# Spreading the softmax's inverse sums by TensorE transposes of a widened copy instead of broadcast DMAs

## The chip, the cores and the metric

The kernel runs on one core of a Trainium2 chip. The metric is device time in microseconds (us) of one execution; for the kernel before, the median of three runs is 564.24 us (563.70 to 567.82). Profiles are single executions recorded by the hardware profiler. PE is TensorE's matmul row and PEld its weight loads, DVE is VectorE, ACT ScalarE, POOL GpSimd, SP SyncE (here it only issues DMAs; SPq is its queue).

## The reference

An attention with a window feeds a gated feed-forward block (FFN). There are 4 batches, 8 heads, 768 positions, head width 64; a query sees the 8 first keys and the 96 last ones.

```python
scores = scale * q @ k.T + bias          # bias: -slope of the head * distance
scores = where(keep, scores, -1e9)
a = exp(scores - max(scores))
a = a / (sum(a) + 1e-9)
x = a @ v                                # heads side by side: [4, 768, 512]
h = relu(x @ w_in)                       # 512 -> 1024
gate = sigmoid(conv3(h))                 # three taps along the positions, per channel
out = (h * gate) @ w_out                 # 1024 -> 512
```

What the change touches is the division by the row sums. The kernel does not divide `a`; it multiplies the product with `v` by the inverse sums. That product stands with the 64 columns of a head on the partitions and the queries along the free axis, so the inverse sums, which come out one per partition (one per query), must be turned, and repeated over 64 partitions.

## The kernel before, in words

**Jobs and steps.** A job `m` is one batch, one half `u` of the positions (384 queries) and one pair of heads: 32 jobs. A job has NB = 3 steps of 128 queries, so there are 96 steps `s`. Four jobs make one FFN stage `n` (8 stages of 384 positions).

**One step of attention.** `scores` (L373) multiplies queries and keys on TensorE into a bank of PSUM (pool `ps_s`, three banks). `maxima` (L408) adds the bias and takes the extremes on DVE. `exps` (L425) takes exponentials on ACT, with the sums of the rows in `sums[m]`. Two steps later (LAG_T) `transposes` (L454) turns the exponentials on TensorE into a bank of pool `ps_t` (one bank), and ACT copies them to SBUF (L464 to L467). After a job's third step `inverses` (L436) adds 1e-9 and takes reciprocals on DVE (128x6). `spread` (L441) transposes these 6 columns on TensorE (L443), copies the 6 rows to SBUF on ACT (`row`, L445) and issues six DMAs from SP (L449), each of which writes one row of 128 numbers to 64 partitions of `rs`. `values` (L470), three steps after a job's last (LAG_V), does 24 small matmuls with `v` (L475), then multiplies by `rs` on DVE (L486) and splits the result into a rounded part `xh` on ACT (L487) and the rest `xl` on POOL (L488). The FFN's first matmuls read those.

**FFN work.** `ffn(n)` (L637) makes a list of items: 24 of `mm1` (four matmuls each, L506), 16 or 32 of `mm2` (three each, L619) of the stage before, and between them the work of the other engines (ReLU L517/L519, three taps L555 to L557, tanh L575, a check of saturation L586, gating and split L607 to L610). The main loop (from L751) takes items from that list by `fill`, some before `values` and `transposes` of a step and some behind. How many is set by `left`, the number of steps to spread the rest of the list over (L798). `fill` puts an item behind the scores, maxima and exponentials of the step before, on each engine.

**Order.** Up to step 10 (HAND = 11) the order on every engine is the order of the program. From step 11 on the compiler's list scheduler, which plans with its own durations, orders ACT, DVE, POOL and SP; TensorE keeps the order of the program (L787). Each engine then works its list strictly in order.

**Beside it.** In the first 15 steps (NATIVE = 5 jobs) each of the two heads of a step has a bank of its own for its scores. In the first 31 steps or so the weights are decoded from 8-byte words on DVE (L318 to L322), in pieces given out per step. `load`, `load_v` and `weight_load` issue the inputs' DMAs from SP. `prep` (L122) rounds the keys and queries of jobs from 5 on, on DVE, ACT and POOL (L134 to L145). At the end `check_weights` (L336) reads the weights once more, in 18 pieces, behind the last `xh` (`cur["mixed"]`) on ACT.

Of the kernel before, what the change touches and what calls it, by code (L numbers as in the profile page):

```python
# [67 lines left out]
def fast_path(tc, io):  # L68
# [14 lines left out]
    pg = pool("pg", 4)  # L83
    ps_s = pool("ps_s", 3, space=PSUM)
    ps_t = pool("ps_t", 1, space=PSUM)
    ps_v = pool("ps_v", 1, space=PSUM)
# [6 lines left out]
    def load(m):  # L93
# [5 lines left out]
        if m < NATIVE:  # L99
            rk = p2.tile([P, w // 2], F32, tag="kk", name=f"rk{m}")  # L100
            rq = p2.tile([P, TB], F32, tag="qh", name=f"rq{m}")
            for j in range(2):
                rows = slice(64 * j, 64 * j + 64)
                k0 = 2 * TB + j * NKC[u]
                nc.sync.dma_start(rk[rows], src[rows, k0 : k0 + NKC[u]])
                nc.sync.dma_start(rq[rows], src[rows, j * TB : (j + 1) * TB])
        else:
            rk = p1.tile([P, w], F32, tag="rk", name=f"rk{m}")
            rq = p1.tile([P, 2 * TB], F32, tag="rq", name=f"rq{m}")
            nc.sync.dma_start(rk, src[:, 2 * TB :])  # L110
            nc.sync.dma_start(rq, src[:, : 2 * TB])
# [258 lines left out]
    last_ttr = {}  # L370
    st_s, st_pt, pv, xt, sums, rs, line = {}, {}, {}, {}, {}, {}, {}

    def scores(s):  # L373
# [9 lines left out]
        else:  # L383
            sp = [ps_s.tile([P, 256], F32, tag="s", name=f"s{s}_{j}") for j in range(2)]
        for j in range(2):
# [22 lines left out]
    def maxima(s):  # L408
# [4 lines left out]
        if i == 0:  # L413
            sums[m] = p1.tile([P, 3, 2 * NB], F32, tag="sums", name=f"sums{m}", bufs=3)
        for j in range(2):
# [9 lines left out]
    def exps(s):  # L425
# [3 lines left out]
        for j in range(2):  # L429
            last_exp[s] = A.activation(  # L430
                pb[:, j, c0 : c0 + n], sp[j][:, c0 : c0 + n], AF.Exp,
                bias=mm[:, j : j + 1], scale=-1.0, accum_out=sums[m][:, 0, NB * j + i : NB * j + i + 1],
            )
# [7 lines left out]
    def spread(m):  # L441
        pv[m] = ps_v.tile([P, TB + P], F32, tag="v", name=f"pv{m}")
        T.transpose(pv[m][: 2 * NB, TB:], sums.pop(m)[:, 2], ident)  # L443
        row = p1.tile([2 * NB, P], F32, tag="row", name=f"row{m}")
        A.activation(row, pv[m][: 2 * NB, TB:], AF.Copy)  # L445
        rs[m] = p2.tile([P, TB], F32, tag="rs", name=f"rs{m}")
        for c in range(2 * NB):
            j, i = divmod(c, NB)
            nc.sync.dma_start(  # L449
                rs[m][64 * j : 64 * j + 64, i * P : (i + 1) * P],  # L450
                row[c : c + 1].unsqueeze(1).broadcast_to([1, D, P]),
            )

# [15 lines left out]

    def values(m):  # L470
        for i in range(NB):
            sb, ka = st_pt.pop(NB * m + i)
            for c, n in ((0, ka), (1, P - 24)):
                for j in range(2):
# [5 lines left out]
                        stop=c == 1,  # L480
                    )
        xh = px.tile([P, TB], F32R, tag="xh", name=f"xh{m}")
        xl = px.tile([P, TB], F32R, tag="xl", name=f"xl{m}")
        xt[m] = (xh, xl)
        x = rs.pop(m)
        V.tensor_tensor(x, pv[m][:, :TB], x, ALU.mult)  # L486
        cur["mixed"] = A.activation(xh, x, AF.Copy)  # L487
# [265 lines left out]
    for s in range(len(steps) + LAG_V + 1):  # L753
        cur["s"] = s
        m, i = steps[s] if s < len(steps) else (len(jobs), -1)
        if s < HAND:
            scores(s)
            if ends(s - LAG_V):
                values((s - LAG_V) // NB)
            if s >= LAG_T:  # L760
                transposes(s - LAG_T)
            maxima(s)
            exps(s)
            if i == 0 and m:
                inverses(m - 1)
            elif i == 1 and m:
                spread(m - 1)
# [15 lines left out]
        else:  # L783
            if hand:
                hand = False
                manual.__exit__(None, None, None)
                manual = tc.manual_schedule(engines={mybir.EngineType.PE})  # L787
                manual.__enter__()
            if s < len(steps):
# [5 lines left out]
            if e >= 0:  # L795
                if e % SPU == SPU - 1:
                    queue.extend(ffn(e // SPU))
                left = SPU - (e + 1) % SPU  # L798
                if e + 1 >= len(steps) - SPU:
                    left += 2  # L800
                k = -(-sum(cost for cost, _, _ in queue) // left)
            if s <= len(steps) and i < 1:
                inverses((s - 1) // NB)
            elif s == len(steps) + 1 or i == 1:
                spread(s // NB - 1)
            if s < LAG_V + SPU:
# [3 lines left out]
            if ends(s - LAG_V):  # L810
                values((s - LAG_V) // NB)
            if s < len(steps) + LAG_T:
                transposes(s - LAG_T)
# [7 lines left out]
        if s == 0:  # L821
            for k in range(len(order)):
                chain(*order[k])
        for k, at in enumerate(FIRST_LOADS):
            if at == s:
                start_piece(k)
        if i == 0:
            prep(m + 1, 0)
            prep(m + 1, 1)
            if 1 <= m < NATIVE - 1:  # L830
                load(m + 1)
        elif i == 1 and m + 2 >= NATIVE:
            load(m + 2)
        if s >= 2 and (s - 2 - (LAG_V - 3)) % NB == 0:
            load_v((s - 2 - (LAG_V - 3)) // NB + 1)
    fill(10**9)
# [6 lines left out]
    last_tiles()  # L843
    manual.__exit__(None, None, None)
    if wide:
# [166 lines left out]
```

## Time and profile before

| | |
|---|---|
| median of three runs | 564.24 us (563.70 to 567.82) |
| the profiled execution's own time | 566.89 us |
| its span, first to last instruction | 565.1 us |
| mean granted TensorE clock | 0.914 |
| time around the span | 566.89 - 565.1 = 1.79 us |

The page of the profile gives busy shares of each engine, the chain of work that ended last (followed back from the last instruction, at each step to what released it), and groups of instructions with their busy time, mean duration, the idle time before them and what ended it. Views of the trace give waits by engine and window, busy time by window, and single instructions in order of time. An engine's idle time costs something only when that engine, or what waits for it, sets the end.

### The profile page before, as it was taken

To read this page: it belongs to the slowest core of one execution; us is meant where nothing else is said; L and a number is where in the kernel's file an instruction comes from. 1 tells how busy PE (TensorE), PEld (TensorE's weight loads), DVE (VectorE), ACT (ScalarE), POOL (GpSimd) and SP (SyncE) were. 2 spreads that over 40 slices of the span, in tenths; PEclk is the share of its full clock that TensorE was granted. 3 is DMA by queue.
4 is the path that set the end of the run, shared out by engine and by line. 5 is a ranking of instruction groups with operands and counts; after the bars stand their busy time and mean duration, and the time that the engine had idled before them with its cause. 6 is when DMAs were issued, how large, how long until landed. Compare 5 with 4: busy or idle time off the path is not lost.

```text
span 565.1 us, 9158 instructions
## 1 busy us (share of the span) xinstructions
PE 474.3 (84%) x3045; PEld 405.1 (72%) x3045; DVE 373.5 (66%) x825; ACT 303.9 (54%) x825; POOL 257.9 (46%) x210
## 2 busy tenths in 40 slices
PE   7686686676967899998978899899978899988795
PEld 6464465575965689787867798788867788777584
DVE  5346599996796758754867788557669677137720
ACT  2345475665756556652565646644655487246710
POOL 4023477663873745673554355574534442233000
PEclk8957688887997979998998899999979899999999
DMA  6844876645553644465555654475545534476511
GB/s 193 200 93 106 186 216 181 139 125 127 101 115 22 149 89 96 115 139 117 107 107 108 143 90 81 78 169 127 109 55 129 118 44 78 82 209 197 179 57 43
DMA packets 38328, 68.10 MB, mean 121 GB/s; under 512 B 6145, under 2 KB 19969, under 8 KB 38273
## 3 DMA queue, kind: packets, MB, share of 16 engines
q1 hardware_dynamic: 34816, 61.28, 50.5%
q10 hardware_dynamic: 3456, 6.16, 2.9%
q8 instruction: 26, 0.43, 0.3%
q14 instruction: 30, 0.24, 0.1%
HBM read 54.84 MB, written 6.29 MB: 108 GB/s over the span
## 4 chain that ended last, share of the span: by engine, by line
DMA 22%; DVE 22%; PE 22%; SPq 12%; ACT 11%; issue 8%; POOL 2%; DVEq 0%; ACTq 0%; POOLq 0%
DMA rs<-row 15%; SPq L449 11%; PE h L506 9%; PE o L619 7%; DVE c L557 3%; DMA check<-in_w_in 3%; DVE c L556 3%; ACT pbuf L430 3%; DVE s L418 3%; DVE c L607 2%; DMA check<-in_w_out 2%; DVE rs L486 2%; DVE w L320 2%; ACT sat L586 1%; PE s L399 1%
## 5 line engine op out<-in xcount | busy, mean ns | idle before, releaser
L430 ACT ACTIVATE pbuf<-s,mm 128x232 f32<-128x232 f32 (+1 forms) x192 | 82.1, 433 | 68.5 <-DVE mm L418 66.7
L555 POOL TENSOR_SCALAR c<-hbuf,cw 128x382 f32<-128x382 f32 (+1 forms) x64 | 47.7, 748 | 78.7 <-ACT hbuf L519 41.4
L619 PE MATMUL o<-woh,gh 128*128 128x512 f32 x192 | 82.5, 430 | 0.8 <-ACT hbuf L519 0.7
L418 DVE CUSTOM_DVE_ANT_0 s<-s,tab 128x232 f32<-128x232 f32 (+1 forms) x192 | 73.0, 385 | 15.2 <-PE s L399 8.2
L619 PE MATMUL o<-woh,gl 128*128 128x512 f32 x192 | 78.4, 408 | 2.9 <-DVE gl L610 2.9
L619 PE MATMUL o<-wol,gh 128*128 128x512 f32 x192 | 78.4, 408 | 0.0
L506 PE MATMUL h<-xh,wih 128*128 128x384 f32 x252 | 60.3, 358 | 18.6 <-ACT xh L487 15.0
L460 PE MATMUL t<-ident,pbuf 128*128 128x128 f32 (+1 forms) x192 | 55.6, 311 | 23.7 <-ACT pt L467 17.2
L488 POOL TENSOR_TENSOR xl<-rs,xh 128x384 fp32r<-128x384 f32 x32 | 37.8, 1180 | 81.0 <-ACT xh L487 74.8
L145 POOL TENSOR_TENSOR ql<-rq,qh 128x768 fp32r<-128x768 f32 x24 | 48.3, 2011 | 44.3 <-DVE qh L140 23.8
L143 POOL TENSOR_TENSOR kk<-rk,kk 64x1008 fp32r<-64x1008 f32 (+1 forms) x27 | 61.0, 2260 | 11.8 <-POOL ql L145 4.5
L556 DVE SCALAR_TENSOR_TENSOR c<-hbuf,cw,c 128x382 f32<-128x382 f32 (+1 forms) x64 | 52.0, 815 | 19.6 <-POOL c L555 19.3
L506 PE MATMUL h<-xl,wih 128*128 128x384 f32 x252 | 62.0, 370 | 0.2 <-POOL xl L488 0.2
L506 PEld LDWEIGHTS h<-xh,wih 128*128 128x128 f32 x252 | 45.9, 199 | 22.1 <-ACT xh L487 17.1
L506 PE MATMUL h<-xh,wil 128*128 128x384 f32 x252 | 61.4, 369 | 0.0
L467 ACT ACTIVATE pt<-t 128x512 f32<-128x512 f32 x80 | 47.1, 589 | 22.0 <-PE t L461 22.0
L475 PE MATMUL pv<-pt,v 104*64 104x128 f32 (+2 forms) x768 | 55.1, 289 | 2.4 <-ACT row L445 1.5
L557 DVE SCALAR_TENSOR_TENSOR c<-hbuf,cw,c 128x382 f32<-128x382 f32 (+1 forms) x64 | 54.9, 858 | 0.8
L460 PEld LDWEIGHTS t<-ident,pbuf 128*128 128x128 f32 (+1 forms) x192 | 27.7, 144 | 38.5 <-ACT pt L467 21.3
L475 PEld LDWEIGHTS pv<-pt,v 104*64 104x64 f32 (+2 forms) x768 | 43.4, 141 | 15.1 <-issue 6.2
L486 DVE TENSOR_TENSOR rs<-pv,rs 128x384 f32<-128x384 f32 x32 | 17.7, 553 | 54.6 <-DMA rs<-row 50.8
L461 PE MATMUL t<-ident,pbuf 128*128 128x128 f32 x192 | 53.2, 299 | 0.0
(112 smaller groups left out, 990.4 us busy)
## 6 DMA issues: line engine op xcount, KB each, us to landing
v<-in_vv SPq DMA_DIRECT2D x32, 384.0 KB, 4.2
rq<-in_qk SPq DMA_DIRECT2D x27, 384.0 KB, 4.0
rk<-in_qk SPq DMA_DIRECT2D x15, 504.0 KB, 3.6
rs<-row SPq DMA_DIRECT2D x192, 32.0 KB, 4.6
out<-ob ACTq DMA_DIRECT2D x23, 256.0 KB, 2.1
rk<-in_qk SPq DMA_DIRECT2D x12, 408.0 KB, 3.8
wr<-in_w_in SPq DMA_DIRECT2D x8, 512.0 KB, 5.5
wr<-in_w_out SPq DMA_DIRECT2D x8, 512.0 KB, 4.4
```

Source lines behind the costliest of these rows:

```text
L143: G.tensor_tensor(kk[64:], rk[64:], kk[64:].bitcast(F32), ALU.subtract)
L145: X.tensor_tensor(ql, rq, qh.bitcast(F32), ALU.subtract)
L418: last_ttr[s] = V.tensor_tensor_reduce(out=sp[j][:, c0 : c0 + n], in0=sp[j][:, c0 : c0 + n], in1=tb, scale=-0.125, scalar=3.0e38, op0=ALU. ...
L430: last_exp[s] = A.activation(pb[:, j, c0 : c0 + n], sp[j][:, c0 : c0 + n], AF.Exp, bias=mm[:, j : j + 1], scale=-1.0, accum_out=sums[m][:, ...
L449: nc.sync.dma_start(rs[m][64 * j : 64 * j + 64, i * P : (i + 1) * P], row[c : c + 1].unsqueeze(1).broadcast_to([1, D, P]),)
L460: T.transpose(pt[:ka, j, 0, :], pb[:, j, c0:P], ident)
L461: T.transpose(pt[:, j, 1, :], pb[:, j, P:256], ident)
L475: T.matmul(pv[m][64 * j : 64 * j + 64, i * P : (i + 1) * P], vt[m][:n, i, c, 64 * j : 64 * j + 64], sb[:n, j, c, :], start=c == 0, stop=c ...
L506: T.matmul(ps[:, :TB], w_[:, k, fs], x_, start=part == 0 and k == 0, stop=part == 2 and k == NK - 1,)
L556: V.scalar_tensor_tensor(c, *tap(0), c, ALU.mult, ALU.add)
L557: V.scalar_tensor_tensor(c, *tap(2), c, ALU.mult, ALU.add)
L619: T.matmul(ps, g_[:, f], w_[:, f], start=f == 0 and part == 0, stop=f == NF - 1 and part == 2,)
```

## The change

**Spread.** `spread` becomes one POOL copy that repeats each inverse sum 64 times along the free axis (`wide`, 128 x 3 x 2 x 64 numbers), in the step in which `inverses` runs. A new `turned` transposes the three 128x128 blocks of `wide` on TensorE behind `values`, into a bank of `ps_t`, and copies 128x384 to `rs` on ACT. The transpose of 6 columns, the copy `row` and the six DMAs of each job go. The sums' tile is laid out by step, then head.

**A step later.** The multiplication and the split move from `values` to a new `mixed`, called in the next step: behind `maxima` and `exps` of that step.

**Banks.** `ps_s` goes from three banks to two, `ps_t` from one to two. In the native steps the second head's scores move from `ps_s` to a bank of `ps_m`, which the FFN's products use as well (three banks). `pv` is taken in `values` and no longer in `spread`.

**Order and pace.** From step 11 on TensorE is ordered by the scheduler too. `left` gets one step more, so a stage's list runs on into the first step of the next one. `load(2)` is issued at step 1 into buffers of its own, `load(3)` and `load(4)` a job earlier, and `load_v(m)` at the first step of each job.

```diff
-    ps_s = pool("ps_s", 3, space=PSUM)
-    ps_t = pool("ps_t", 1, space=PSUM)
+    ps_s = pool("ps_s", 2, space=PSUM)
+    ps_t = pool("ps_t", 2, space=PSUM)
...
-            sp = [ps_s.tile([P, 256], F32, tag="s", name=f"s{s}_{j}") for j in range(2)]
+            other = ps_m.tile([P, 512], F32, tag="m", name=f"s{s}_1")
+            sp = [ps_s.tile([P, 256], F32, tag="s", name=f"s{s}_0"), other]
...
     def spread(m):
-        pv[m] = ps_v.tile([P, TB + P], F32, tag="v", name=f"pv{m}")
-        T.transpose(pv[m][: 2 * NB, TB:], sums.pop(m)[:, 2], ident)
-        row = p1.tile([2 * NB, P], F32, tag="row", name=f"row{m}")
-        A.activation(row, pv[m][: 2 * NB, TB:], AF.Copy)
-        rs[m] = p2.tile([P, TB], F32, tag="rs", name=f"rs{m}")
-        for c in range(2 * NB):
-            j, i = divmod(c, NB)
-            nc.sync.dma_start(
-                rs[m][64 * j : 64 * j + 64, i * P : (i + 1) * P],
-                row[c : c + 1].unsqueeze(1).broadcast_to([1, D, P]),
-            )
+        inv = sums.pop(m)[:, 2]
+        wide = p2.tile([P, NB, 2, D], F32, tag="wide", name=f"wide{m}", bufs=1)
+        G.tensor_copy(wide, inv.unsqueeze(3).broadcast_to([P, NB, 2, D]))
+        wides[m] = wide.rearrange("p i j d -> p i (j d)")
+
+    def turned(m):
+        wide = wides.pop(m)
+        pt = ps_t.tile([P, 2, 2, P], F32, tag="t", name=f"rt{m}")
+        flat = pt.rearrange("p j c q -> p (j c q)")[:, :TB]
+        for i in range(NB):
+            T.transpose(flat[:, i * P : (i + 1) * P], wide[:, i], ident)
+        rs[m] = p2.tile([P, TB], F32, tag="rs", name=f"rs{m}", bufs=1)
+        A.activation(rs[m], flat, AF.Copy)
...
+
+    def mixed(m):
         xh = px.tile([P, TB], F32R, tag="xh", name=f"xh{m}")
         xl = px.tile([P, TB], F32R, tag="xl", name=f"xl{m}")
         xt[m] = (xh, xl)
         x = rs.pop(m)
-        V.tensor_tensor(x, pv[m][:, :TB], x, ALU.mult)
+        V.tensor_tensor(x, pv[m], x, ALU.mult)
...
-                manual = tc.manual_schedule(engines={mybir.EngineType.PE})
-                manual.__enter__()
...
-                left = SPU - (e + 1) % SPU
+                left = SPU - (e + 1) % SPU + 1
                 if e + 1 >= len(steps) - SPU:
-                    left += 2
+                    left += 1
...
+            if ends(e):
+                mixed(e // NB)
             if s <= len(steps) and i < 1:
                 inverses((s - 1) // NB)
-            elif s == len(steps) + 1 or i == 1:
-                spread(s // NB - 1)
+                spread((s - 1) // NB)
...
             if ends(s - LAG_V):
                 values((s - LAG_V) // NB)
+                turned((s - LAG_V) // NB)
```

More of the change, by code (lines that the diff above doesn't have):

```diff
@@ L99, in load @@
         if m < NATIVE:
-            rk = p2.tile([P, w // 2], F32, tag="kk", name=f"rk{m}")
-            rq = p2.tile([P, TB], F32, tag="qh", name=f"rq{m}")
+            rk = (p1 if m == 2 else p2).tile([P, w // 2], F32, tag="rk" if m == 2 else "kk", name=f"rk{m}")
+            rq = p2.tile([P, TB], F32, tag="ql" if m == 2 else "qh", name=f"rq{m}")
             for j in range(2):
@@ L370, in fast_path @@
     last_ttr = {}
-    st_s, st_pt, pv, xt, sums, rs, line = {}, {}, {}, {}, {}, {}, {}
+    st_s, st_pt, pv, xt, sums, rs, wides = {}, {}, {}, {}, {}, {}, {}
     def scores(s):
@@ L413, in maxima @@
         if i == 0:
-            sums[m] = p1.tile([P, 3, 2 * NB], F32, tag="sums", name=f"sums{m}", bufs=3)
+            sums[m] = p1.tile([P, 3, NB, 2], F32, tag="sums", name=f"sums{m}", bufs=3)
         for j in range(2):
@@ L431, in exps @@
                 pb[:, j, c0 : c0 + n], sp[j][:, c0 : c0 + n], AF.Exp,
-                bias=mm[:, j : j + 1], scale=-1.0, accum_out=sums[m][:, 0, NB * j + i : NB * j + i + 1],
+                bias=mm[:, j : j + 1], scale=-1.0, accum_out=sums[m][:, 0, i, j : j + 1],
             )
@@ L470, in values @@
     def values(m):
+        pv[m] = ps_v.tile([P, TB], F32, tag="v", name=f"pv{m}")
         for i in range(NB):
@@ L763, in fast_path @@
             exps(s)
+            if ends(s - LAG_V - 1):
+                mixed((s - LAG_V - 1) // NB)
             if i == 0 and m:
                 inverses(m - 1)
-            elif i == 1 and m:
                 spread(m - 1)
@@ L811, in fast_path @@
                 values((s - LAG_V) // NB)
+                turned((s - LAG_V) // NB)
             if s < len(steps) + LAG_T:
@@ L823, in fast_path @@
                 chain(*order[k])
+        elif s == 1:
+            load(2)
         for k, at in enumerate(FIRST_LOADS):
@@ L829, in fast_path @@
             prep(m + 1, 1)
-            if 1 <= m < NATIVE - 1:
-                load(m + 1)
+            if 1 <= m < NATIVE - 2:
+                load(m + 2)
         elif i == 1 and m + 2 >= NATIVE:
             load(m + 2)
-        if s >= 2 and (s - 2 - (LAG_V - 3)) % NB == 0:
-            load_v((s - 2 - (LAG_V - 3)) // NB + 1)
+        if s >= NB and i == 0:
+            load_v(m)
     fill(10**9)
@@ L843, in fast_path @@
     last_tiles()
-    manual.__exit__(None, None, None)
     if wide:
```

## The prediction

> **What bounds the kernel now.** I read the page first (shares, then the chain that ended last), then busy time by window, then who waited for whom by window, then single stretches of the timeline.
>
> ```profile
> span 565.1 us, 9158 instructions
> ...
> PE 474.3 (84%) x3045; PEld 405.1 (72%) x3045; DVE 373.5 (66%) x825; ACT 303.9 (54%) x825; POOL 257.9 (46%) x210
> ...
> DMA rs<-row 15%; SPq L449 11%; PE h L506 9%; PE o L619 7%; DVE c L557 3%; DMA check<-in_w_in 3%; DVE c L556 3%; ACT pbuf L430 3%; DVE s L418 3%; DVE c L607 2%; DMA check<-in_w_out 2%; DVE rs L486 2%; DVE w L320 2%; ACT sat L586 1%; PE s L399 1%
> ```
>
> No engine is full over the whole span, and a quarter of the chain (15% + 11%) is the spread that the change removes: SP issuing the six broadcasts and their landing. That is 147 us of chain, but a chain's share is no gain: PE may have had work beside it. So I go by stages (start:end, length, then busy us of PE, PEld, DVE, ACT, POOL, granted clock).
>
> ```profile
> 0.00:62.00 62.00, 42.37 (x310) 31.68 (x310) 28.82 (x99) 21.56 (x74) 15.87 (x39) 0.81 0.62 148
> 62.00:130.00 68.00, 50.90 (x331) 43.60 (x331) 64.84 (x121) 45.91 (x120) 48.10 (x32) 0.83 0.65 165
> 200.00:260.00 60.00, 58.65 (x385) 51.61 (x385) 39.28 (x82) 33.61 (x93) 35.10 (x24) 0.96 0.52 102
> 260.00:320.00 60.00, 50.52 (x343) 43.78 (x341) 42.43 (x94) 32.59 (x94) 26.54 (x20) 0.94 0.53 111
> 495.00:535.00 40.00, 32.66 (x157) 27.61 (x157) 23.68 (x54) 24.78 (x59) 8.99 (x10) 1.00 0.69 206
> ```
>
> Up to 62 us nothing is full: waits set the pace. From 62 to 130 DVE is full (64.84 of 68), with the decoding of weights. From 200 on PE is: nearly full in stages with 32 items of mm2 (58.65 of 60), less so in those with 16 (50.52).
>
> Where does the spread hurt? DVE's waits for the broadcasts in the windows 0 to 62 and 62 to 130 (total us, times, longest), then one of them by itself:
>
> ```profile
> DVE rs L486 <- DMA rs<-row: 22.2, 3, 9.0
> ```
> ```profile
> DVE rs L486 <- DMA rs<-row: 6.0, 3, 5.3
> ```
> ```profile
> 18.98 0.68 DVE L322 SCALAR_TENSOR_TENSOR w<-wr,w 128x512 int32<-128x512 int32 x1
> 27.57 0.56 DVE L486 TENSOR_TENSOR rs<-pv,rs 128x384 f32<-128x384 f32 x1 [7.90 <-DMA rs<-row]
> 28.04 0.40 DVE L418 CUSTOM_DVE_ANT_0 s<-s,tab 128x232 f32<-128x232 f32 x1
> ```
> ```profile
> 22.18 0.50 PE L389 MATMUL s<-rk,rq 64*128 64x136 f32 x2
> 29.69 0.59 PE L389 MATMUL s<-rk,rq 64*128 64x136 f32 x1 [7.01 <-ACT pbuf L430]
> ```
>
> The multiplication stands in DVE's list ahead of the next maxima (L418), whose scores PE had written before. So DVE, ACT behind it and PE (7.01 us) all stand. (22.2 less 7.9 and 9.0, the longest, leaves a third of 5.3: the 5.3 that the second window lists too is that one, across the border at 62, and I count it once.) In the hand-ordered part this happens in three jobs, 22.2 us, with nothing beside it.
>
> **The change part by part.** *Spread.* Per job it removes and adds:
>
> ```profile
> L449 SPq DMA_DIRECT2D rs<-row x192: 463/594/1495, 19.5 to 489.6; - x192
> ...
> DMA to landing us min/median/max: 3.2/4.6/6.1
> ```
> ```profile
> L519 ACT ACTIVATE hbuf<-h 128x384 f32<-128x384 f32 x50 | 24.2, 483 | 8.2 <-PE h L506 8.2
> L555 POOL TENSOR_SCALAR c<-hbuf,cw 128x386 f32<-128x386 f32 x32 | 24.0, 752 | 40.4 <-ACT hbuf L519 20.4 <-DVE hbuf L517 20.0
> L445 ACT ACTIVATE row<-pv 6x128 f32<-6x128 f32 x32 | 8.2, 256 | 14.1 <-PE pv L443 14.1
> ```
> ```profile
> 307.31 0.27 PE L461 MATMUL t<-ident,pbuf 128*128 128x128 f32 x1
> 307.42 0.27 PE L460 MATMUL t<-ident,pbuf 128*128 128x128 f32 x1
> 307.53 0.27 PE L461 MATMUL t<-ident,pbuf 128*128 128x128 f32 x1
> ```
>
> SP loses 6 x 0.594 = 3.6 us of issuing and 4.6 us to landing: some 8 us between the sums and the multiplication. PE: a 128x128 transpose takes 0.11 us of PE's stream (307.31, 307.42, 307.53); the old one streams 128 columns too, so PE gets 3 - 1 = 2 more, 0.22 us a job. ACT: a copy of 128x384 (0.483) for `row` (0.256): 0.23 us more a job, 7 us in all, on an engine at 54%. POOL: no row shows a copy that reads one number 64 times. The nearest is a 128x386 operation with one input, 0.75 us; I bound it below by zero and above by twice that, 1.5 us. I take 0.75, so 24 us over the run on an engine at 46%. It runs two steps ahead of `turned`, so its own latency is hidden; if it weren't, 0.75 a job in the hand part, 2 us. In the new order the multiplication waits for three transposes and one ACT copy, 0.33 + 0.48 us, instead of SP and the DMAs, and it stands a step later.
>
> *POOL against DVE.* POOL work can stretch DVE's casts:
>
> ```profile
> L140 DVE CAST qh<-rq x22: 551/560/2702, 134.8 to 449.1; 128x768 fp32r<-128x768 f32 x22
> ```
>
> The same cast takes 0.551 at best and 2.702 at worst. Where DVE is the bound (62 to 130 and some way beyond, about ten jobs of 14 us), ten copies of 0.75 us may so hold DVE up: 0 to 7.5 us, and I take 2 net of the small waits that go there. Here the Trainium skill speaks against the change: SBUF — State Buffer, section "Who interferes with whom", says that GpSimd and some VectorE operations (casts, or two inputs in SBUF) share a port pair under an exclusive lock, and that the second one blocks fully. The row agrees in kind (2.702 against 0.551); by that rule alone, with every copy meeting such an operation, the term would be the full 7.5 us instead of 2.
>
> *Hand-ordered part, to 62 us.* The 22.2 us go, and per job 0.33 (transposes) + 0.48 (copy) + 0.56 (a multiplication now behind other maxima) = 1.4 us may come back: 22.2 - 3 x 1.4 = **-18** (bounds -22 to -8, the latter if PE's or the weights' own pace takes over). The stall hid nothing that can't run elsewhere: the decoding that stands behind it is a fixed amount per step. The early loads go past SP's broadcasts, which are gone.
>
> *62 to 130.* DVE is full; its 64.84 us remain. **+2** (bounds -4 to +8).
>
> *130 to 495.* What TensorE itself waits for in this window is what an edit can give back:
>
> ```profile
> PE h L506 <- ACT xh L487: 15.0, 7, 3.4
> PE t L460 <- ACT pt L467: 10.7, 7, 3.4
> PE pv L443 <- DVE sums L439: 8.1, 1, 8.1
> PE t L460 <- ACT pt L465: 6.3, 5, 1.6
> ```
> ```profile
> 497.16 0.40 PE L619 MATMUL o<-woh,gl 128*128 128x512 f32 x1
> 497.39 0.87 PE L506 MATMUL h<-xh,wih 128*128 128x384 f32 x4
> 498.10 0.87 PE L506 MATMUL h<-xl,wih 128*128 128x384 f32 x4
> ```
>
> The first, 2.1 us a time, is PE at the start of a stage waiting for the last `xh`. A thirteenth of the stage's work now stands ahead of it: 24 + 16 (or 32) items of about 0.7 us each (four matmuls of mm1 start 0.71 us before the next four, and one of mm2, of which an item has three, 0.23 before the next matmul) is 28 or 39 us, a thirteenth 2.2 or 3.0. I credit 12 of 15.0. The waits of the transposes (17.0) are for their only bank; the second one gives some step more, but ACT that is late for other reasons stays late: 10. The wait of the 6-column transpose for the sums goes with it, and `turned` has two steps' margin: 6 of 8.1. That is 28; since a PE that arrives earlier meets other waits (DVE's casts, ACT behind the maxima), I take three quarters, 21. Against it, 25 jobs x 0.22 = 5.5 us more work for PE. **-15.5** (bounds -34.6, all 40.1 gone, to +5.5, all back elsewhere).
>
> *Two score banks.* Cost nil in my sum: the third use of a bank must wait for the exponentials two steps before, and these were done. In the tightest stretch I looked at:
>
> ```profile
> 304.94 0.27 PE L399 MATMUL s<-kk,qh 128*128 128x232 f32 x1
> ...
> 311.16 0.44 ACT L430 ACTIVATE pbuf<-s,mm 128x232 f32<-128x232 f32 x1
> ...
> 312.81 0.27 PE L399 MATMUL s<-kk,qh 128*128 128x232 f32 x1
> ```
>
> A step's scores start at 304.94, its exponentials end at 311.6, and the scores two steps later start at 312.81: 1.2 us to spare. If the cover goes, each late step costs PE its lateness, with the FFN's matmuls queued behind. *TensorE's order*: nothing of the trace shows what the planner would choose; I take 0 for both, bounds in the rivals: down to 500 us in all by (b), up to 577 by (d). *Loads and v*: issued earlier or a step later, on an SP queue with 114 us less issuing (192 x 0.594): 0.
>
> *The end.* The last multiplication waits 8.45 us:
>
> ```profile
> 493.59 0.56 DVE L486 TENSOR_TENSOR rs<-pv,rs 128x384 f32<-128x384 f32 x1 [8.45 <-DMA rs<-row]
> ```
>
> Yet PE has mm2 to do until 497.39, by the rows above, and takes up the FFN products that need it only there. What the last `xh` also releases is the check of the weights on ACT, which then shares DVE and ACT with the last stage (495 to 535, where PE is busy 32.66 of 40): **-2** (0 to -8).
>
> Sum: -18 + 2 - 15.5 - 2 = -33.5 us. Against the profiled execution, 565.1 + 1.79 = 566.89, that is 533.4. This execution lay 2.65 above the median, so against 564.24 I forecast **531 us**.
>
> **Rivals.** One row of the waits of the whole run first, ACT's exponentials behind DVE's maxima:
>
> ```profile
> ACT pbuf L430 <- DVE mm L418: 66.7, 35, 6.3
> ```
>
> (a) *Only the stalls of the hand part go*; from 130 on what TensorE stops waiting for, it waits for elsewhere (these 66.7 us are more than any term above). Then -18 + 2 + 5.5 - 2: 564.2 - 12.5 = 552. For it: DVE and ACT feed each other in order; against it: PE is nearly full in half of the stages.
>
> (b) *The scheduler orders TensorE better than the program did*, and nearly all named waits go: -22 - 4 - 34.6 - 4 = -65, 500 us. For it: every wait of PE is one of being in a fixed order with other work at hand. Against: it plans with its own durations, and casts that take 0.55 or 2.7 can't be planned.
>
> (c) *No change*: the 18 us of the hand part are taken back between 62 and 150 by DVE, whose decoding is fixed, or by the weights' loads, and the rest cancels: about 560.
>
> (d) *Slower: score banks.* The free order hoists each step's scores to the moment when the planner believes a bank is free, ahead of FFN items; on the chip the exponentials are later than planned, and PE stands there with the FFN behind. Place: PE at L399, 84 steps from step 11 on. It decides from 33.5 / 84 = 0.40 us a step; at 0.55 us it costs 46 us, and the time is 564.2 - 33.5 + 46 = 577. For it: only 1.2 us to spare in the stretch above, and a spread of DVE's durations larger than that. Against: PE's program order had room there, and items are not allowed more than one step ahead.
>
> (e) *It doesn't do what it says*: the 8 us reappear as DVE waiting for ACT's copy of `rs`, because ACT is behind. That is (a) or (c) in effect.
>
> **How the numbers follow.** Chances: the forecast 0.55, (a) 0.17, (b) 0.11, (c) with (e) 0.08, (d) 0.09. A measurement of this kernel tells about 1% from no change (5.6 us, 558.6 to 569.9). Faster by over 1%: 0.55 + 0.17 + 0.11 = 0.83; within 1%: 0.08; slower: 0.09. The forecast's own bounds are wide (-22 - 4 - 34.6 - 8 to -8 + 8 + 5.5), but these do not all fall together; its own range is 512 to 548. The range for 8 in 10 takes in (a) with some margin and most of (b): 505 to 557.
>
> **What would show it.** Right: the waits of L486's successor for a DMA gone, and none above 2 us in its place before 50 us; the stretch in which DVE is full (from 62 us) begins 15 to 20 us earlier; stages with 16 items of mm2 down from 60 us to 55 or less, those with 32 hardly changed; PE's busy time up by about 7 us (32 x 0.22); waits for `xh` at the stages' starts below 5 us in all. Wrong: PE idle at L399 behind ACT's exponentials (d); a DVE share above 95% from 40 to 130 with the same end (c); POOL's copy over 1.5 us.

## The result, and the profile after

The changed kernel takes 522.74 us (median of 4 runs, 522.24 to 527.32) against 565.33 us before (median of 4 runs in this comparison): a ratio of 0.9261, 95% interval 0.9197 to 0.9326. The forecast was 531, its range 505 to 557. The profiled execution took 522.24 us.

The page, in the rows that answer to those shown before (span, busy time, chain by line):

```profile
span 520.5 us, 8853 instructions
...
PE 467.4 (90%) x3109; PEld 397.7 (76%) x3109; DVE 381.5 (73%) x825; ACT 310.8 (60%) x825; POOL 281.5 (54%) x242
...
PE o L625 17%; PE h L512 8%; DVE c L562 6%; PE pv L479 6%; DVE c L563 4%; DVE s L419 4%; PE s L400 4%; DVE c L613 3%; DMA check<-in_w_out 3%; DMA check<-in_w_in 2%; DVE kk L136 2%; ACT pbuf L431 2%; DVE w L322 2%; PE t L463 2%; DVE w L318 2%
```

The spread is gone from the chain (it was 15% and 11%); TensorE's lines lead it now. (Lines have moved by one to six: L419 is the maxima, L431 the exponentials, L463 and L464 the transposes, L479 the small matmuls, L512 mm1, L625 mm2, L492 the multiplication.)

To see where the 44.6 us of span went I cut both executions where TensorE starts the scores of steps 11, 27, 51, 63 and 75, read from the timeline: windows of busy time again (start:end, length, PE, PEld, DVE, ACT, POOL, granted clock). First some of the kernel before, then the same stretches of the changed one.

```profile
0.00:52.10 52.10, 36.62 (x266) 27.96 (x266) 25.22 (x90) 18.17 (x62) 14.41 (x38) 0.77 0.63 159
52.10:129.10 77.00, 55.74 (x372) 46.71 (x372) 67.87 (x127) 48.68 (x130) 48.67 (x32) 0.84 0.64 157
...
259.30:317.60 58.30, 50.14 (x342) 43.72 (x341) 41.54 (x91) 31.79 (x91) 24.89 (x20) 0.94 0.51 107
317.60:380.10 62.50, 58.85 (x390) 51.29 (x389) 42.59 (x93) 36.02 (x99) 36.02 (x24) 0.97 0.55 113
```
```profile
0.00:34.10 34.10, 28.48 (x277) 22.49 (x278) 23.88 (x87) 18.21 (x61) 17.76 (x41) 0.98 0.77 232
34.10:109.30 75.20, 57.64 (x381) 46.21 (x377) 63.93 (x125) 48.27 (x126) 51.67 (x38) 0.83 0.43 147
...
234.00:284.00 50.00, 49.06 (x352) 42.72 (x351) 39.49 (x88) 31.91 (x91) 28.89 (x24) 1.00 0.36 109
284.00:345.60 61.60, 59.27 (x395) 52.23 (x394) 48.76 (x98) 37.80 (x100) 36.73 (x29) 0.97 0.33 101
```

Read row against row: the hand-ordered part is 18.0 us shorter (52.1 to 34.1), the stretch with the decoding 1.8 (77.0 to 75.2), a stage with 16 items of mm2 8.3 (58.3 to 50.0, and TensorE is now busy 49.06 of 50), one with 32 items 0.9. From step 27 to the end it is 436.0 to 411.2, 24.8 us. TensorE's busy time in that stretch hardly changed (381.97 to 381.27, the number behind the length in these rows, before and after), so nearly all of the 24.8 us is time in which it had stood idle:

```profile
129.10:565.10 436.00, 381.97 (x2411) 330.39 (x2409) 280.38 (x610) 237.06 (x634) 194.84 (x140) 0.94 0.51 109
```
```profile
109.30:520.50 411.20, 381.27 (x2456) 328.99 (x2454) 293.68 (x614) 244.30 (x638) 212.08 (x164) 0.97 0.34 104
```

The hand-ordered part, DVE's timeline around the first multiplication:

```profile
22.07 0.34 DVE L419 CUSTOM_DVE_ANT_0 s<-s,tab 128x136 f32<-128x136 f32 x1
22.33 0.14 DVE L419 DVE_READ_ACCUMULATOR2_ANT mm<- 128x1 f32 x1
22.33 0.55 DVE L492 TENSOR_TENSOR rs<-pv,rs 128x384 f32<-128x384 f32 x1
22.79 0.16 DVE L439 TENSOR_SCALAR sums<-sums 128x6 f32<-128x6 f32 x1
```

No bracket, so no wait, where 7.90 us stood. And what TensorE waits for from step 27 on, its six longest (`issue` is idle time before which the profile shows nothing that was waited for):

```profile
PE pv L479 <- issue: 5.4, 1, 5.4
PE h L512 <- ACT xh L493: 4.7, 2, 2.3
PE s L400 <- ACT pbuf L431: 3.5, 1, 3.5
PE t L463 <- ACT pbuf L431: 2.7, 1, 2.7
PE o L625 <- ACT gh L614: 2.3, 2, 1.9
PE t L463 <- ACT pt L468: 1.9, 2, 0.9
```

The four rows of the prediction held 40.1 us there; the wait for the transposes' bank (17.0) is down to some 2, that for `xh` from 15.0 to 4.7, and the wait for the sums is gone.

### The profile page after: what moved, and what is told of

It reads as the page before. It is cut to its first block, busy times and chain, and to the rows that moved or that the text cites. A ratio compares the mean times of both kernels' runs of the same rounds, so it can differ in the third digit from the quotient of the medians.

```text
span 520.5 us, 8853 instructions
## 1 busy us (share of the span) xinstructions
PE 467.4 (90%) x3109; PEld 397.7 (76%) x3109; DVE 381.5 (73%) x825; ACT 310.8 (60%) x825; POOL 281.5 (54%) x242
## 4 chain that ended last, share of the span: by engine, by line
PE 40%; DVE 32%; ACT 10%; DMA 8%; issue 5%; POOL 2%; SPq 1%; ACTq 0%; POOLq 0%; DVEq 0%
PE o L625 17%; PE h L512 8%; DVE c L562 6%; PE pv L479 6%; DVE c L563 4%; DVE s L419 4%; PE s L400 4%; DVE c L613 3%; DMA check<-in_w_out 3%; DMA check<-in_w_in 2%; DVE kk L136 2%; ACT pbuf L431 2%; DVE w L322 2%; PE t L463 2%; DVE w L318 2%
## 5 line engine op out<-in xcount | busy, mean ns | idle before, releaser
L431 ACT ACTIVATE pbuf<-s,mm 128x232 f32<-128x232 f32 (+1 forms) x192 | 82.7, 437 | 81.1 <-DVE mm L419 73.4
L419 DVE CUSTOM_DVE_ANT_0 s<-s,tab 128x232 f32<-128x232 f32 (+1 forms) x192 | 72.9, 387 | 34.5 <-PE s L400 27.1
L625 PE MATMUL o<-woh,gh 128*128 128x512 f32 x192 | 79.4, 413 | 2.6 <-ACT gh L614 2.3
L561 POOL TENSOR_SCALAR c<-hbuf,cw 128x382 f32<-128x382 f32 (+1 forms) x64 | 51.5, 811 | 53.0 <-ACT hbuf L525 38.8
L625 PE MATMUL o<-wol,gh 128*128 128x512 f32 x192 | 77.0, 401 | 0.0
L625 PE MATMUL o<-woh,gl 128*128 128x512 f32 x192 | 76.7, 400 | 0.0
L479 PE MATMUL pv<-pt,v 104*64 104x128 f32 (+2 forms) x768 | 63.0, 294 | 13.3 <-issue 5.4
L479 PEld LDWEIGHTS pv<-pt,v 104*64 104x64 f32 (+2 forms) x768 | 44.9, 142 | 31.3 <-issue 14.5
L562 DVE SCALAR_TENSOR_TENSOR c<-hbuf,cw,c 128x382 f32<-128x382 f32 (+1 forms) x64 | 57.1, 903 | 15.7 <-POOL c L561 15.5
L512 PE MATMUL h<-xh,wih 128*128 128x384 f32 x252 | 61.4, 361 | 6.4 <-ACT xh L493 4.7
L563 DVE SCALAR_TENSOR_TENSOR c<-hbuf,cw,c 128x382 f32<-128x382 f32 (+1 forms) x64 | 61.7, 972 | 0.6
L463 PE MATMUL t<-ident,pbuf 128*128 128x128 f32 (+1 forms) x192 | 51.1, 290 | 9.7 <-ACT pt L470 3.1
L512 PE MATMUL h<-xl,wih 128*128 128x384 f32 x252 | 58.9, 347 | 0.0
L512 PE MATMUL h<-xh,wil 128*128 128x384 f32 x252 | 55.1, 340 | 0.0
L400 PE MATMUL s<-kk,qh 128*128 128x232 f32 (+1 forms) x162 | 44.2, 295 | 10.8 <-ACT pbuf L431 10.8
L512 PEld LDWEIGHTS h<-xh,wih 128*128 128x128 f32 x252 | 45.9, 200 | 9.0 <-ACT xh L493 5.1
L616 POOL TENSOR_TENSOR gl<-c,gh 128x1024 fp32r<-128x1024 f32 (+2 forms) x16 | 36.3, 2276 | 26.6 <-ACT gh L614 20.2
L464 PE MATMUL t<-ident,pbuf 128*128 128x128 f32 x192 | 49.6, 282 | 0.4 <-POOL pbuf L282 0.4
L494 POOL TENSOR_TENSOR xl<-rs,xh 128x384 fp32r<-128x384 f32 x32 | 36.9, 1154 | 20.7 <-ACT xh L493 16.4
## 6 DMA issues: line engine op xcount, KB each, us to landing
wr<-in_w_in SPq DMA_DIRECT2D x8, 512.0 KB, 5.7
wr<-in_w_out SPq DMA_DIRECT2D x8, 512.0 KB, 3.7
```

What stands on the lines that cost most here:

```text
L400: last_mm[s] = T.matmul(sp[j][:, c0 : c0 + n], q_[:, j * TB + i * P : j * TB + (i + 1) * P], kk[:, j * w + k0 : j * w + k0 + n], start=st, ...
L419: last_ttr[s] = V.tensor_tensor_reduce(out=sp[j][:, c0 : c0 + n], in0=sp[j][:, c0 : c0 + n], in1=tb, scale=-0.125, scalar=3.0e38, op0=ALU. ...
L431: last_exp[s] = A.activation(pb[:, j, c0 : c0 + n], sp[j][:, c0 : c0 + n], AF.Exp, bias=mm[:, j : j + 1], scale=-1.0, accum_out=sums[m][:, ...
L463: T.transpose(pt[:ka, j, 0, :], pb[:, j, c0:P], ident)
L464: T.transpose(pt[:, j, 1, :], pb[:, j, P:256], ident)
L479: T.matmul(pv[m][64 * j : 64 * j + 64, i * P : (i + 1) * P], vt[m][:n, i, c, 64 * j : 64 * j + 64], sb[:n, j, c, :], start=c == 0, stop=c ...
```

## Experiments

The open question was which part of the change did it. My theory was the prediction's: the spread clears the hand-ordered part, and the second bank and the longer pace take TensorE's waits away behind it, its order being worth little. The main rival gave the later gain to the free order. For each run the table has when TensorE starts the scores of steps 11, 27 and 95 and the end of the span, in its profiled execution, and the ratio of times to the kernel before. Each ratio is taken against runs of the kernel before in the same session (medians of 562.5 to 565.4 us), so it isn't quite the median over 565.3.

| run | step 11 | step 27 | step 95 | end | median us | ratio, 95% interval |
|---|---|---|---|---|---|---|
| before | 52.0 | 129.1 | 475.5 | 565.1 | 565.3 | |
| after | 34.1 | 109.3 | 434.6 | 520.5 | 522.7 | 0.926 (0.920 to 0.933) |
| e1_order | 30.0 | 105.9 | 435.0 | 523.3 | 525.4 | 0.931 (0.924 to 0.938) |
| e3_spread | 36.1 | 110.4 | 441.1 | 529.8 | 531.5 | 0.941 (0.933 to 0.948) |
| e6_same_step | 36.9 | 110.5 | 438.6 | 526.2 | 530.4 | 0.946 (0.943 to 0.949) |
| e4_dma_later | 40.9 | 120.3 | 464.6 | 554.5 | 557.0 | 0.986 (0.979 to 0.994) |
| e5_free | 54.0 | 125.6 | 452.2 | 537.1 | 539.1 | 0.955 (0.948 to 0.962) |
| e7_banks_alone | 49.5 | 127.7 | 466.2 | 557.6 | 557.4 | 0.991 (0.987 to 0.995) |
| e8_pace | 35.7 | 112.0 | 430.5 | 519.5 | 519.2 | 0.924 (0.918 to 0.929) |
| e2_banks | 33.4 | 108.4 | 477.4 | 571.2 | 573.3 | 1.023 (1.019 to 1.028) |
| e12_shared | 34.0 | 104.5 | 453.2 | 532.7 | 535.1 | 0.949 (0.942 to 0.957) |
| e10_own_bank | 32.9 | 110.0 | 432.7 | 516.7 | 518.0 | 0.919 (0.914 to 0.924) |
| e11_wide_act | 33.0 | 104.8 | 424.8 | 513.9 | 516.1 | 0.915 (0.909 to 0.921) |
| e9_late_free | 30.6 | 105.3 | 419.2 | 506.6 | 512.0 | 0.909 (0.905 to 0.914) |

A caution for all of them: from step 11 on each kernel is planned anew, so an edit changes the order of everything behind it. A few us between two runs can be the plan's.

**e1_order: the change without the free order.**

```diff
                 manual.__exit__(None, None, None)
+                manual = tc.manual_schedule(engines={mybir.EngineType.PE})
+                manual.__enter__()
```

> The changed kernel with TensorE kept in program order from step 11 on, as before; all else as changed. Theory (the spread, the second bank for the transposes and the longer pace take TensorE's waits away, and its order is worth little): 523 to 532 us. Rival (the free order is what shortens the stages from step 27 on): those 21 us come back, 540 to 547 us, with TensorE again waiting ahead of the transposes; step 11 still starts near 34 us in both.

525.4 us: the theory's side. With the new spread in place the order is worth 2.7 us by the medians, and the two intervals overlap. TensorE's waits from step 27 on:

```profile
PE t L463 <- ACT rs L455: 11.2, 7, 2.6
PE h L512 <- ACT xh L493: 7.4, 5, 3.1
PE s L400 <- ACT pbuf L431: 4.1, 2, 2.8
```

Up to step 27 program order is even earlier (105.9 against 109.3), behind it slower (417.4 against 411.2). The first row is new: the transposes now wait for the turned copy, which shares their banks.

**e3_spread: the spread, a step later, and the banks; no free order, old pace, old loads.** The edit is the diff shown without its blocks on `manual` and `left`, put on the kernel before with its old loads. (The banks come with it, since the turned copy takes one of the transposes' banks.)

> The kernel before with the new spread, applied a step later, and with two and two banks; TensorE in program order, the old pace and the old loads. Theory: the 18 us of the hand-ordered part and a good part of the 21 behind it, 530 to 545 us. Rival (free order): only the hand-ordered part, 545 to 550 us. Rival (loads and pace matter): over 550 us.

531.5 us, 34 of the 43 us, as the theory had it: 18.7 up to step 27 and 16.6 behind.

e1_order differs from this run only by the early loads and the new pace, and takes 6.0 us less by the medians (the intervals overlap a little). So 565.4 goes to 531.5 with spread and banks, to 525.4 with loads and pace, to 522.7 with the free order. Up to step 10 both runs have the same order, and the pace doesn't act yet; e1_order starts step 10 at 29.44 us, this run at 35.26, the kernel before at 49.73. What TensorE waits for there in this run, then in e1_order, are the loads of the queries:

```profile
PE s L390 <- DMA rq<-in_qk: 5.2, 3, 3.8
```
```profile
PE s L390 <- DMA rq<-in_qk: 0.6, 1, 0.6
```

So the early loads are worth some 6 us by step 10; 4.5 of the difference are left at step 27 (110.4 to 105.9).

**e6_same_step: as e3_spread, applied at once** (in the hand-ordered part and behind it; the diff shows one place).

```diff
                 turned((s - LAG_V) // NB)
-            if ends(e):
-                mixed(e // NB)
+                mixed((s - LAG_V) // NB)
```

> As the run with the spread alone (531.5 us), but multiplied and split in the same step, right behind the three transposes and their copy. Theory (the new path from the sums to the multiplication is under 2 us, so being a step later matters little): 530 to 537 us. Rival (the step later is what hides the path): DVE waits at each multiplication for TensorE's small matmuls, transposes and ACT's copy, 3 to 4 us a job where DVE sets the pace, 540 to 550 us.

530.4 us, no different from 531.5: with the old loads, being a step later is worth nothing that can be measured. It does what one would think to DVE:

```profile
DVE rs L492 <- ACT rs L455: 20.1, 8, 9.8
```

The same row of the changed kernel:

```profile
DVE rs L492 <- ACT rs L455: 9.9, 2, 9.5
```

DVE waits 20.1 us instead of 9.9, and the run is no longer for it than e3_spread. A single wait of over 9 us in each run is the last job's, during which TensorE has other work (in the changed kernel it is busy for 9.60 of the 9.60 us). Up to step 11 DVE waits 6.4 us here, in a stretch in which e3_spread waits for its loads instead (0.8 us of that here), and both reach step 11 at nearly the same time. What a step later is worth with the early loads was not run.

**e4_dma_later: the DMAs kept, applied a step later** (again in two places, of which the diff shows the first).

```diff
+            if ends(s - LAG_V - 1):
+                mixed((s - LAG_V - 1) // NB)
```

> The kernel before with the broadcast DMAs kept and only the multiplication and split moved a step later. Theory (8 us of issuing and landing are longer than a step of the hand-ordered part, some 3.5 us): DVE still waits 3 to 6 us a job there, and 552 to 560 us come out. Rival (being a step later is enough, the DMAs needn't go): DVE's waits for the broadcasts vanish, 535 to 547 us.

557.0 us, as the theory had it. DVE in the first 62 us:

```profile
DVE rs L488 <- DMA rs<-row: 10.4, 3, 4.4
```

Half of 22.2 is left: 8 us of issuing and landing against a step of some 3.5 us here (an estimate: 40.9 us over 11 steps is 3.7). Step 11 starts 11.1 us earlier and most of that remains at the end (10.6); from step 27 to the end it takes 434.2 us against 436.0. Being later alone gives about a fifth of the change's gain (1.4% of 7.4% by the ratios).

**e5_free: only the free order.**

```diff
-                manual = tc.manual_schedule(engines={mybir.EngineType.PE})
-                manual.__enter__()
```

> The kernel before with TensorE's order left to the scheduler from step 11 on and nothing else. Theory (order worth little): 558 to 568 us. Rival (free order is what gives the 21 us from step 27 on): 540 to 548 us. If it is harmful by itself: over 570 us, with TensorE at the scores waiting for exponentials.

539.1 us: here the theory is wrong and the rival right (1 us below its range). Nothing is gained up to step 11 (54.0 against 52.0). DVE still waits for the broadcasts there, in the first 62 us:

```profile
DVE rs L486 <- DMA rs<-row: 17.2, 2, 9.2
```

But from step 27 to the end it takes 411.5 us, as short as the changed kernel's 411.2. What TensorE waits for there:

```profile
PE pv L443 <- DVE rs L486: 13.6, 5, 3.9
PE o L619 <- ACT gh L608: 2.0, 2, 1.4
PE pv L475 <- ACT pt L467: 2.0, 3, 1.3
PE t L460 <- ACT pt L467: 0.9, 2, 0.5
```

With one bank for the transposes and broadcasts that land late, the waits for `xh` (15.0) and for that bank (17.0) are gone or below 1 us, so the free order found other work to put ahead of them. Either remedy takes most of them, and both together no more than the free order alone: from step 27 to the end it is 436.0 us with neither, 419.4 with spread and banks (e3_spread), 411.5 with the free order, 411.2 with all.

**e7_banks_alone: only two and two banks.** The edit is the first two blocks of the diff.

> The kernel before with two banks for scores and two for transposes and nothing else. Theory (the second bank takes most of the 17 us of waits ahead of the transposes away, and two score banks are enough): 552 to 560 us, nothing gained up to step 27. Rival (the broadcasts, not the bank, are behind those waits, since ACT that is late stays late): 562 to 567 us. Rival (two score banks hurt): over 570 us.

557.4 us, in the theory's range, and 6.1 us less from step 27 on (436.0 to 429.9) for a wait of 17. TensorE from step 27 on:

```profile
PE h L507 <- ACT xh L488: 17.9, 7, 3.3
PE pv L444 <- DVE sums L440: 7.1, 3, 2.4
PE s L400 <- ACT pbuf L431: 5.7, 2, 5.2
```

The waits ahead of the transposes are gone, and others have grown: for `xh` (15.0 to 17.9) and at the scores (none to 5.7), in a fixed order that must wait somewhere. The prediction gave the bank 10 of the 17 and three quarters of that, 7.5 us. Two score banks did no harm that shows in the time.

**e8_pace: the changed kernel with the old pace.**

```diff
-                left = SPU - (e + 1) % SPU + 1
+                left = SPU - (e + 1) % SPU
...
-                    left += 1
+                    left += 2
```

> The changed kernel with the old pace (a stage's list ends with its last step). Theory (a thirteenth of the stage's work covers the wait for the last xh, 15 us of waits before and 4.7 after): TensorE waits some 2 us longer at each of 7 starts of stages, 530 to 537 us. Rival (a free order finds other work there anyway): 521 to 526 us.

519.2 us: the rival's side. The thirteenth of work that I credited with 12 us is worth nothing under a free order (by the medians 3.5 less without it, inside the intervals). The waits of this run have no row for `xh` at all. In program order, the order for which I credited it, e1_order has the new pace and e3_spread the old one: from step 27 on 417.4 us against 419.4, and the waits for `xh` and `xl` there come to 9.4 us (7.4 + 2.0) against 11.1 (5.6 + 5.5). So there it is worth some 2 us at most.

**e2_banks: the changed kernel with three banks for scores and one for all transposes.**

```diff
-    ps_s = pool("ps_s", 2, space=PSUM)
-    ps_t = pool("ps_t", 2, space=PSUM)
+    ps_s = pool("ps_s", 3, space=PSUM)
+    ps_t = pool("ps_t", 1, space=PSUM)
```

> The changed kernel with three banks for scores and one for transposes, as before (the turned copy shares that one). Theory, as the free-order run left it (with TensorE's order free, a wait for the transposes' bank is filled with FFN work): 521 to 527 us. Rival (the second bank carries part of the gain in any order): 530 to 538 us, with TensorE waiting for ACT's copies ahead of the transposes. Rival (two score banks cost something): under 520 us.

573.3 us, 2% slower than the kernel before (1.9% to 2.8%), and further off than any expectation. Up to step 27 it is as early as the change (108.4); behind it every stage is longer. ACT, whole run:

```profile
ACT pbuf L431 <- PE t L464: 66.9, 39, 5.0
ACT rs L455 <- PE rt L453: 45.7, 23, 5.5
```

In the changed kernel the first row reads:

```profile
ACT pbuf L431 <- PE t L464: 4.5, 1, 4.5
```

The exponentials wait for a buffer (there are three) until the transposes of three steps before have read it: the transposes come late. That is not the whole loss: of the 51.6 us that this run is longer from step 27 on, TensorE is idle for 18.7 (48.6 against 29.9) and busy for 32.9 (414.2 against 381.3, at a granted clock of 0.93 against 0.97). Why the same work takes it longer was not found.

**e10_own_bank: one bank for the transposes, one for the turned copy.**

```diff
-    ps_t = pool("ps_t", 2, space=PSUM)
+    ps_t = pool("ps_t", 1, space=PSUM)
+    ps_r = pool("ps_r", 1, space=PSUM)
```

> The changed kernel with one bank for the transposes of the exponentials and one of its own for the turned copy (two for scores, as changed). With three score banks and one bank for both, 573 us came out. Theory (there the turned copy, which waits for POOL and for its place in the order, held the one bank and kept the transposes back): with a bank apart 520 to 530 us. Rival (a single bank for the transposes is what costs 50 us when the order is free): 555 to 575 us. Between: 535 to 550 us, both.

518.0 us, 2 us below the theory's range: a single bank for the exponentials' transposes costs nothing, provided that the turned copy has another.

**e12_shared: both in one bank, two score banks.**

```diff
-    ps_t = pool("ps_t", 2, space=PSUM)
+    ps_t = pool("ps_t", 1, space=PSUM)
...
-    ps_m = pool("ps_m", 3, space=PSUM)
+    ps_m = pool("ps_m", 4, space=PSUM)
```

> The changed kernel with one bank that the transposes of the exponentials and the turned copy share, two score banks as changed, and the bank that this frees given to the FFN's products (four). Theory (sharing one bank is what made 573 us of three score banks and one shared bank): 560 to 580 us, ACT's exponentials waiting for late transposes. Rival (the third score bank did it, the planner running scores ahead): 515 to 530 us.

535.1 us, between both expectations.

```profile
ACT pbuf L431 <- PE t L464: 54.5, 32, 4.3
ACT pbuf L431 <- DVE mm L419: 34.9, 14, 6.3
```

Sharing brings the late transposes (54.5 us of waits, near the 66.9) and 12 us of time, whatever the FFN's fourth bank gave included. The other 38 us of e2_banks come with the bank that went from the FFN's products to the scores; whether the scores' third or the FFN's missing fourth does it wasn't told apart. Here too most of it is TensorE busy for longer (395.2 us from step 27 on, against 381.3), not idle (33.0 against 29.9).

**e11_wide_act: the widening on ACT.**

```diff
-        G.tensor_copy(wide, inv.unsqueeze(3).broadcast_to([P, NB, 2, D]))
+        A.activation(wide, inv.unsqueeze(3).broadcast_to([P, NB, 2, D]), AF.Copy)
```

> The changed kernel with the widening copy on ACT instead of POOL. Theory (POOL's copies of 0.5 us now and then hold a DVE operation up, at most 7.5 us over the run, and ACT at 60% has room): 519 to 526 us. Rival (the shared port costs DVE much: its time per tap grew from 0.84 to 0.94 us): under 517 us. Rival (ACT, in order behind the exponentials, is late with the copy): 528 to 540 us.

516.1 us. By the medians that is 6.6 less, on the side of the first rival, but the two ratios' intervals touch (0.920 to 0.933, 0.909 to 0.921), and e10_own_bank, which keeps the copies on POOL, is as fast (0.914 to 0.924). The two taps on DVE in the changed kernel, in this run and in e10_own_bank (busy us, mean ns):

```profile
L563 DVE SCALAR_TENSOR_TENSOR c<-hbuf,cw,c 128x382 f32<-128x382 f32 (+1 forms) x64 | 61.7, 972 | 0.6
L562 DVE SCALAR_TENSOR_TENSOR c<-hbuf,cw,c 128x382 f32<-128x382 f32 (+1 forms) x64 | 57.1, 903 | 15.7 <-POOL c L561 15.5
```
```profile
L563 DVE SCALAR_TENSOR_TENSOR c<-hbuf,cw,c 128x382 f32<-128x382 f32 (+1 forms) x64 | 59.7, 935 | 0.7
L562 DVE SCALAR_TENSOR_TENSOR c<-hbuf,cw,c 128x382 f32<-128x382 f32 (+1 forms) x64 | 53.5, 838 | 23.2 <-POOL c L561 23.1
```
```profile
L563 DVE SCALAR_TENSOR_TENSOR c<-hbuf,cw,c 128x382 f32<-128x382 f32 (+1 forms) x64 | 56.2, 885 | 14.1 <-POOL c L562 14.0
L564 DVE SCALAR_TENSOR_TENSOR c<-hbuf,cw,c 128x382 f32<-128x382 f32 (+1 forms) x64 | 51.2, 808 | 0.9
```

With the copies on ACT the taps take 5.6 us of 118.8 less; with them on POOL and another plan (e10_own_bank) they take 11.4 less. So what POOL's copies cost DVE is not shown by this run: it lies within what a new plan changes.

**e9_late_free: the faster version that these point to.** The old pace (the edit of e8_pace), and TensorE in program order up to step 26, free behind it.

```diff
+                manual = tc.manual_schedule(engines={mybir.EngineType.PE})
+                manual.__enter__()
+            if s == 27:
+                manual.__exit__(None, None, None)
```

> The changed kernel with the old pace and with TensorE in program order until step 26, free from step 27 on. Up to step 27 program order took 105.7 us, the free one 109.0 and 111.8; behind it the free order took 405.5 and 401.7, program order 411.9. Theory (the two stretches add up): 105.7 + 402 and 7 around them, 512 to 516 us. Rival (what is early at step 27 is lost again where TensorE is full): 519 to 523 us, as with the old pace alone.

512.0 us (508.4 to 515.4): the stretches add up. (The expectation's 405.5, 401.7 and 411.9 end some 6 us before the span does, and its 7 adds that back.) Its interval (0.905 to 0.914) lies clear of the changed kernel's (0.920 to 0.933). It reaches step 27 at 105.3 us, and takes 401.3 from there.

## Why the prediction was right, and where its reasons were not

By its own steps, in the profiled executions (span 565.1 to 520.5, 44.6 us; forecast 33.5):

- **Hand-ordered part, -18: the mechanism was right, and the size (18.0) in part luck.** The prediction put three waits there, 22.2 us. Two of them stand before step 11, which starts at 52.0 us; with the first at 27.57 us (7.90), the other two are:

```profile
44.40 0.56 DVE L486 TENSOR_TENSOR rs<-pv,rs 128x384 f32<-128x384 f32 x1 [9.02 <-DMA rs<-row]
61.70 0.56 DVE L486 TENSOR_TENSOR rs<-pv,rs 128x384 f32<-128x384 f32 x1 [5.31 <-DMA rs<-row]
```

By its own working the part was thus worth 16.9 - 2 x 1.4 = 14.1 us, and the spread without the early loads (e3_spread) starts step 10 by 14.5 us and step 11 by 15.9 us earlier. The rest is the early loads: the step "*Loads and v*: issued earlier or a step later ...: 0" was wrong, since they bring step 10 forward by another 5.8 us (e1_order). A shorter path alone brings step 11 forward by 15.1 us (e6_same_step), a later multiplication alone by 11.1 (e4_dma_later): these two are remedies for one wait as well. e5_free has both waits left (17.2 us) and gains nothing up to step 11, where the order is fixed.
- **62 to 130, +2: measured -1.8** between steps 11 and 27, within the bounds, with the third of those waits in it. DVE stayed the busiest engine there (63.93 of 75.2 us after, 67.87 of 77.0 before); that its fixed work sets the time fits this, but was not tested by itself.
- **POOL's copy, 0.75 us taken:** its row gives 0.506 (median) and 1.496 (longest); the copy of `rs` on ACT, taken as 0.483, took 0.491:

```profile
L445 POOL COPY wide<-sums x32: 504/506/1496, 16.4 to 441.1; 128x384 f32<-128x384 f32 x32
```
```profile
L455 ACT ACTIVATE rs<-rt x32: 464/491/519, 20.0 to 450.4; 128x384 f32<-128x384 f32 x32
```

The Trainium skill's rule (SBUF — State Buffer, "Who interferes with whom": an operation of VectorE with two inputs in SBUF and one of GpSimd that reads SBUF shut each other out) is neither borne out nor refuted for these copies by a run here: the taps changed more with the plan (118.8 to 107.4 us in e10_own_bank) than with the copies off POOL (118.8 to 113.2 in e11_wide_act). The 2 taken for it and the 7.5 worked out by it both stay open.
- **From step 27 on, -15.5 and -2 for the end: measured -24.8.** The stages came out as forecast, 16 items from 58.3 to 50.0 and 32 items nearly the same. What failed is the working inside this term, in three places. First, "A thirteenth of the stage's work now stands ahead of it", credited with 12 us: e8_pace shows 0 in a free order, and e1_order against e3_spread some 2 in program order. The wait for `xh` fell with the spread itself (15.0 to 5.6 in e3_spread, and 5.5 for `xl`). Second, "*TensorE's order*: ... I take 0": by itself the free order gave 24.5 us from step 27 on (436.0 to 411.5). Third, "25 jobs x 0.22 = 5.5 us more work for PE": the 64 matmuls came (3045 to 3109), but TensorE's busy time from step 27 on did not rise (381.97 to 381.27). For the spread and the banks alone, without the pace, the sum's own terms make (10 + 6) x 3/4 - 5.5 + 2 = 8.5 us; e3_spread shows 16.6. So the sum of 17.5 comes to 70% of the measured 24.8 only because a credit that was too high stood for others that were too low or nil: that is luck. The two main remedies, the spread and the free order, clear the same waits; I had added up credits per wait where I should have asked how many ways the waits had to vanish.
- **The transposes' bank, 10 of 17:** the wait went, and by itself the bank brought 6.1 us from step 27 on, near the 7.5 that three quarters make (e7_banks_alone). In the changed kernel its use is to keep the turned copy out of the transposes' way (e10_own_bank against e12_shared).
- **Two score banks, 0:** nothing speaks against it (TensorE's wait for them from step 27 on is 3.5 us in the change, and e7_banks_alone got faster with two); no run changed them alone.
- **Signs.** DVE's wait for a DMA at the multiplication is gone, and no wait stands in its place before 50 us; step 11 starts 18 us earlier; stages with 16 items take 50.0 us; waits for `xh` come to 4.7; POOL's longest copy is 1.496. One sign failed: TensorE's busy time was to rise by 7 us and fell by 6.9 (474.3 to 467.4), with the mean granted clock up from 0.914 to 0.951.
- **Rivals.** (a) failed: the row that it rested on did not shrink (ACT's waits for the maxima, 66.7 to 73.4), and TensorE's idle time from step 27 on still fell from 54.0 to 29.9 us. (b) was right on the order, and its 500 us was not reached: TensorE is busy for 381 of the 411 us from step 27 on. (c), (d) and (e) did not occur in the change (DVE's wait for the copy of `rs` is 9.9 us, 9.5 of them for the last job); e2_banks shows that a planned order can cost 50 us when banks are dealt out badly, though with three score banks and not with two.

## What to carry to other kernels

A transfer that stands in an engine's list can cost its whole length beyond the slack in that list, however little it moves: 8 us of issuing and landing made waits of 7.9 and 9.0 us, and of 3.7 and 2.3 with a step of slack. Three transposes and two copies a job (0.33 + 0.51 + 0.49 = 1.3 us by their rows) took its place. When several edits can each fill the same idle time, measure them one by one and together: 34 us (spread and banks) and 26 us (free order) made 43. Measure the edits that were counted as nothing too: the early loads were worth some 6 us by step 10. After handing an engine's order to a planner, look at every shared buffer again: one bank shared by two users cost 12 us with the freed bank given to the FFN, and 50 with it given to the scores.

## What the runs showed of the hardware that was not expected

- The granted clock rose as waits went: from 0.94 to 1.00 in the stage with 16 items shown above, where TensorE did more instructions (352 against 342) in less busy time (49.06 against 50.14 us). Before, the longest single wait in that stage was 3.4 us (for the transposes' bank); after, it was 0.9. The Trainium skill, TensorE: Matmul & The Clock Gate, "Part 1: The HAM clock gate", states that the clock drops after an idle window of about 3.4 us. The rows agree as far as they go, since the longer waits went with the lower clock; no run here set the length of a wait by itself.
- POOL's copy that reads one number 64 times took 0.506 us for 128x384 (median), and ACT's took 0.522 in e11_wide_act. POOL's operation with one input of 128x386 separate numbers, from which the prediction took its 0.75, is another operation (0.752 us before).
